# Linear attention followed by a channel mix on one core: first batch in two halves up to the channel mix, tail groups in one PSUM tile, loads in pieces

## The chip, the cores and the metric

The kernel runs on one core of a Trainium2 chip. The metric is the device time of one execution in microseconds (us). A kernel is given by the median of its runs; a ratio is the mean time of one kernel's fast runs over the mean of the other's fast runs of the same rounds on the same chip, so it is not quite the ratio of the medians that stand beside it. A run more than 1.5% above the fastest of its kernel counts as slow and is left out of ratios. Intervals are 95%.

## The reference

```python
def phi(x):                                   # q, k: [8, 8, 576, 64], w_phi: [64, 128]
    proj = x @ w_phi
    proj = proj - max(abs(proj), axis=-1)
    return concatenate([exp(proj), exp(-proj)])
kv  = phi(k).T @ v                            # per head; z = sum of phi(k) over the sequence
x   = (phi(q) @ kv) / (phi(q) @ z)            # heads side by side: [8, 576, 512]
# channel mix
x_prev = x shifted by one position
xk = mu_k * x + (1 - mu_k) * x_prev           # xr the same with mu_r
out = sigmoid(xr @ w_r) * (relu(xk @ w_k) ** 2 @ w_v)
```

There are 8 batches, and 4 pairs of heads in each, so 32 pairs; 576 positions are nine slots of 64.

## The kernel before: what the change and the argument touch

The program is a list of named steps, and one long string, ORDER, fixes their order. Each engine executes its own steps in this order. A word is `step:buffer/ENGINE+fillers`; pair numbers stand behind the name, and fillers are matmuls whose result nobody uses, placed where TensorE would stand idle. PSUM is the memory that TensorE writes its products to; a one-bank tile of this program holds 512 columns of it, a two-bank tile 1024. The granted clock is the share of TensorE's full clock that the profile shows as granted. For a pair n the chain is: `qp`, `kp` (projections on TensorE), `rq`, `rk` (maxima on VectorE), `mh` (the maxima split in two bf16 parts), `mt`, `mc` (transposed and copied), `ka`, `qt` (the maxima subtracted on TensorE), `ea`, `eb`, `qa`, `qb` (exponentials on ScalarE), `kv`, `kc`, `nd` (the two attention products), `rd` (division by the denominator, giving x_sc). From pair 8 on, x is transposed by a DMA that SyncE issues (`xz`); `xu`, `df`, `xa`, `xb` then make the shifted copy, the difference and the two mixes. `h`, `r`, `v` are the channel-mix products of a batch, `rl`, `sq`, `th`, `ob`, `so` what follows them. The ninth slots of a batch's pairs form a tail group with its own short chain: `tp`, `rt`, `mhe`, `mte`, `mce`, `kae`, `ekt`, `qte`, `eqe`.

```python
        def mhx():                                        # step mh, on GpSimd
            nc.gpsimd.tensor_copy(mhv[:, :, 0], nmv)
            nc.gpsimd.tensor_tensor(mhv[:, :, 1], nmv, mhv[:, :, 0], op=ALU.subtract)
        ...
        def eq(pn):                                       # steps qa, qb: two instructions of 512 columns each
            ...
                for h in range(2):
                    nc.scalar.activation(t[:, h, :]..., s["qT"]...[:, h], AF.Exp, scale=...)
        ...
        def xz():                                         # SyncE
            nc.sync.dma_start_transpose(out=xs[:, a, :]..., in_=s["x"]...)
        def xu(eng):                                      # GpSimd or VectorE, as ORDER says
            copy(eng, xs[:, a, 1:64], xs[:, a, 576:639])
        ...
        def mte():                                        # tail group: a one-bank tile of its own
            s["pm"] = pm = motile(("mo", "m" + tag), "ps_me")
            nc.tensor.transpose(pm[:, 0:64].bitcast(BF), mh, ident)
        def ekt():                                        # reads bank 0 of the tail group's two-bank tile
            ... nc.scalar.activation(t[:, a0:a1, :], s["ps"][:, 0, 0:n * 128]..., AF.Exp, ...)
        def qte():                                        # writes another one-bank tile
            s["pq"] = ps = motile(("mo", "q" + tag), "ps_qe")
    ...
    lparts = {b: [(0, NP)] for b in range(B)}             # whole-batch loads, from batch 2 on
```

## Time and profile before

| kernel before | value | where it is read |
|---|---|---|
| time | 305.18 us (304.40 to 307.18, 4 runs) | the runs |
| span of the profiled run | 304.2 us | page |
| TensorE idle | 25.8 us | span less busy time |
| granted clock, mean | 0.986 | trace |
| first channel-mix matmul | 51.9 us | timeline of TensorE |

Three more lines of the DMA view matter later, the last of them for pair 8's transpose alone (window 86:87 us). Its columns are output and input, queue, count, size of one, and the median time from issue to landing in us:

```profile
nat<-in_q_dram POOLq DMA_DIRECT2D x6, 576.0 KB, 8.9
xs<-x_sc SPq DMA_TRANSPOSE x24, 3.5
...
xs<-x_sc SPq DMA_TRANSPOSE x1, 2.6
```

A transpose of x takes 3.5 us in the median, and pair 8's, the first, 2.6 us: the last load issued before it had landed at 81.8 us, 4.6 us before its issue. Pair 12's took 11.0 us (issued at 120.48, landed at 131.48). The planned duration in the program text is 2.2 us (the third argument of `op("xz" + N + ".d", "DMA", 2.2, ...)`), and the order was laid out with that.

### The profile page before, as it was taken

The page shows a single profiled execution, that of the slowest core. Times are in us where ns is not written, and L with a number is a line of the kernel's source. Part 1 is how long each engine was busy: PE and PEld are TensorE (multiplying, and loading weights), DVE is VectorE, ACT ScalarE, POOL GpSimd, SP SyncE. Part 2 cuts the span into 40 slices and gives each one's busy share as a digit, 9 for nine tenths or more (in the row PEclk, how much of TensorE's full clock was granted, in tenths as well). Part 3 has the DMA queues.
Part 4 walks back from the last instruction along what each step waited for, and adds up shares of the span by engine and source line. Part 5 has one row for each costly group of instructions (what it writes and reads, how often), then busy time and mean ns, then how long its engine had stood idle before and what let it go on. Part 6 is the DMA issues. An engine that isn't in the chain of part 4 may idle for free.

```text
span 304.2 us, 9054 instructions
## 1 busy us (share of the span) xinstructions
PE 278.4 (92%) x3765; PEld 158.4 (52%) x3813; DVE 240.3 (79%) x369; ACT 223.3 (73%) x408; POOL 127.4 (42%) x261
## 2 busy tenths in 40 slices
PE   6688798999899999969999997999999999999993
PEld 2456465565456655534555654454556655554541
DVE  5776789979978999667978988799869888777331
ACT  3397899998689897855888884898797878923410
POOL 7763533696047346653443714353034403400400
PEclk9999989999999999998999999999999999999999
DMA  8999957399989957996957898913924364233125
GB/s 152 204 209 207 169 83 105 59 194 206 194 174 128 148 124 131 197 200 113 177 110 107 145 125 157 162 47 61 187 60 69 11 93 94 58 74 71 39 58 116
DMA packets 66137, 38.18 MB, mean 126 GB/s; under 512 B 47024, under 2 KB 60720, under 8 KB 66096
## 3 DMA queue, kind: packets, MB, share of 16 engines
q1 hardware_dynamic: 51280, 20.82, 39.4%
q0 software_dynamic: 14672, 16.48, 35.1%
q8 instruction: 30, 0.49, 0.7%
q10 hardware_dynamic: 144, 0.29, 0.3%
q14 instruction: 11, 0.09, 0.1%
HBM read 33.62 MB, written 9.44 MB: 142 GB/s over the span
## 4 chain that ended last, share of the span: by engine, by line
PE 61%; DVE 18%; DMA 7%; ACT 6%; issue 3%; POOL 2%; SPq 1%; DVEq 0%; POOLq 0%
PE ps_v L812 14%; PE ps_h L779 13%; PE ps_r L798 7%; PE ps_nd L656 5%; DMA xs<-x_sc 4%; PE ps_kv L635 4%; DVE nm L565 4%; DVE nm L560 3%; DVE xk L706 2%; PE ps_ve L896 2%; ACT q L620 2%; PE ps_he L866 2%; DVE xr L706 2%; PE ps_q L548 2%; PE ps_k L598 2%
## 5 line engine op out<-in xcount | busy, mean ns | idle before, releaser
L620 ACT ACTIVATE q<-ps_qT 128x512 bf16<-128x512 f32 x128 | 67.1, 622 | 3.0 <-PE ps_qT L612 2.8
L575 ACT ACTIVATE k<-ps_k 128x1024 bf16<-128x1024 f32 x64 | 62.9, 1038 | 5.6 <-PE ps_k L598 4.3
L779 PE MATMUL ps_h<-xk,wk_bf 128*128 128x512 bf16 x237 | 60.8, 379 | 1.3 <-issue 0.3
L812 PE MATMUL ps_v<-wv_bf,kk 128*128 128x512 bf16 x243 | 58.2, 379 | 1.0 <-issue 0.3
L565 DVE TENSOR_REDUCE nm<-ps_q 128x8 f32<-128x1024 f32 x32 | 38.7, 1218 | 4.3 <-PE ps_q L548 4.1
L560 DVE TENSOR_REDUCE nm<-ps_k 128x8 f32<-128x1024 f32 x32 | 38.8, 1217 | 3.8 <-PE ps_k L548 3.8
L812 PEld LDWEIGHTS <-kk 128*128 128x128 bf16 x256 | 23.9, 98 | 28.8 <-issue 1.9
L211 POOL TENSOR_TENSOR kk<-krelu 128x512 bf16<-128x512 bf16 x23 | 23.9, 1047 | 35.4 <-DVE krelu L205 21.7
L779 PEld LDWEIGHTS <-wk_bf 128*128 128x128 bf16 x256 | 22.5, 97 | 25.2 <-issue 2.3
L584 POOL CAST mhl<-nm 128x16 bf16<-128x16 f32 x32 | 8.0, 250 | 64.1 <-DVE nm L560 64.0
L798 PE MATMUL ps_r<-wr_bf,xr 128*128 128x512 bf16 x118 | 32.9, 394 | 1.2 <-issue 0.5
L804 ACT ACTIVATE rt<-ps_r 128x512 bf16<-128x512 f32 x32 | 19.5, 609 | 18.0 <-PE ps_r L798 15.7
L700 POOL TENSOR_TENSOR diff<-xs 128x576 bf16<-128x576 bf16 x21 | 28.0, 1336 | 7.6 <-DVE xs L682 2.8
L203 ACT ACTIVATE krelu<-ps_h 128x512 bf16<-128x512 f32 x39 | 23.2, 611 | 10.1 <-PE ps_h L779 8.3
L706 DVE SCALAR_TENSOR_TENSOR xk<-diff,mu_k_t,xs 128x576 bf16<-128x576 bf16 x32 | 28.5, 892 | 1.3 <-POOL diff L700 1.0
L818 DVE SCALAR_TENSOR_TENSOR ob<-rt,ps_v 128x512 f32<-128x512 bf16 x32 | 21.8, 682 | 8.7 <-PE ps_v L812 4.2
L666 DVE TENSOR_TENSOR x_sc<-ps_nd,rden 128x640 bf16<-128x640 f32 x32 | 26.4, 825 | 1.1
L706 DVE SCALAR_TENSOR_TENSOR xr<-diff,mu_r_t,xs 128x576 bf16<-128x576 bf16 x32 | 26.9, 840 | 0.0
L548 PEld LDWEIGHTS <-qkT 64*128 64x128 bf16 x512 | 17.6, 94 | 12.0 <-issue 9.7
L635 PE MATMUL ps_kv<-v,k 64*128 64x65 bf16 x1024 | 22.8, 192 | 0.6 <-ACT q L620 0.4
L635 PEld LDWEIGHTS <-k 64*128 64x128 bf16 x1024 | 19.9, 95 | 5.1 <-issue 3.8
L205 DVE TENSOR_SCALAR krelu<-ps_h 128x512 bf16<-128x512 f32 x25 | 17.1, 688 | 6.6 <-PE ps_h L779 6.0
(99 smaller groups left out, 467.5 us busy)
## 6 DMA issues: line engine op xcount, KB each, us to landing
out_dram<-ob SPq DMA_DIRECT2D x72, 128.0 KB, 2.4
nat<-in_k_dram POOLq DMA_DIRECT2D x6, 576.0 KB, 8.6
nat<-in_q_dram POOLq DMA_DIRECT2D x6, 576.0 KB, 8.9
vt<-in_v_dram POOLq DMA_DIRECT2D x6, 576.0 KB, 9.6
wk_bf<-in_moe_w_k_dram POOLq DMA_DIRECT2D x2, 512.0 KB, 10.8
wv_bf<-in_moe_w_v_dram POOLq DMA_DIRECT2D x2, 512.0 KB, 12.3
nat<-in_k_dram POOLq DMA_DIRECT2D x3, 288.0 KB, 7.4
nat<-in_q_dram POOLq DMA_DIRECT2D x3, 288.0 KB, 7.3
```

The costliest lines, as they stand in the source:

```text
L211: (nc.vector if eng == "DVE" else nc.gpsimd).tensor_tensor(out_, in_, in_, op=ALU.mult)
L560: nc.vector.tensor_reduce(s["nm"][:, 0, :], s["k"].rearrange("p a (g f) -> p (a g) f", f=128), axis=AX.X, op=ALU.max, apply_absolute_value ...
L565: nc.vector.tensor_reduce(s["nm"][:, 1, :], s["q"].rearrange("p a (g f) -> p (a g) f", f=128), axis=AX.X, op=ALU.max, apply_absolute_value ...
L575: nc.scalar.activation(s[f"k{pn}"], s["k"].rearrange("p a (g f) -> p (a g) f", f=128), AF.Exp, scale=(1.0 if pn == 0 else -1.0))
L620: nc.scalar.activation(t[:, h, :].rearrange("f (g a p) -> f g a p", g=4, a=2), s["qT"].rearrange("f a (g h p) -> f h g a p", g=4, h=2)[:, ...
L635: nc.tensor.matmul(ps[:, hh, pn * 65:(pn + 1) * 65], lhsT=s[f"k{pn}"][r, c, :], rhs=vb[r, a, 2 * g + par, :], start=(pn == 0 and c == 0), ...
L666: nc.vector.tensor_tensor(s["x"].rearrange("p (b s) d -> p b s d", b=2), ndv[:, :, :, 0:64], s["rd"].to_broadcast([128, 2, 5, 64]), op=ALU ...
L700: (nc.vector if eng == "DVE" else nc.gpsimd).tensor_tensor(s["d"], xs[:, a, 64:64 + S], xs[:, a, 0:S], op=ALU.subtract)
L706: nc.vector.scalar_tensor_tensor(out=t[:, a, (b % 2) * S:(b % 2 + 1) * S], in0=s["d"], scalar=mu[:, a:a + 1], in1=xs[:, a, 0:S], op0=ALU.m ...
L779: nc.tensor.matmul(ps, lhsT=wk_bf[:, c, fc * 128:(fc + 1) * 128], rhs=xkt[bp][:, c, m0:m0 + 512], start=(c == 0), stop=(c == NDC - 1))
L798: nc.tensor.matmul(ps, lhsT=xrt[bp][:, c, m0 + ci * 128:m0 + (ci + 1) * 128], rhs=wr_bf[:, c, :], start=(c == 0), stop=(c == NDC - 1))
L812: nc.tensor.matmul(ps, lhsT=s["kk"][:, fc, ci * 128:(ci + 1) * 128], rhs=wv_bf[:, fc, :], start=(fc == 0), stop=(fc == NFC - 1))
```

## The change

The intent was to start the channel mix earlier, by having only the first slots of the first batch done, and to free the two one-bank PSUM tiles from the tail groups. Cut to its core:

```diff
+    NHALF = NP                                  # pairs 0 to 3: qt, qa, qb, nd, rd, xt, xe, df, xa, xb twice,
+            for i, h in enumerate("yz"):        #   "y" for slots 0 to 5, "z" for slots 6 to 9
...
+        def h2(k):                              # batch 0: ps_h of 256 tokens x two blocks of features
...
-                for h in range(2):
-                    nc.scalar.activation(...)   # q exponentials: four of 512 columns in a pair
+                nc.scalar.activation(t..., s["qT"]..., AF.Exp, ...)   # two of 1024
...
         def mte():
-            s["pm"] = pm = motile(("mo", "m" + tag), "ps_me")
+            nc.tensor.transpose(s["ps"][:, 1, 0:64].bitcast(BF), mh, ident)
         def qte():
-            s["pq"] = ps = motile(("mo", "q" + tag), "ps_qe")
+            s["pq"] = ps = s["ps"][:, 1, :]     # bank 1 of the tile whose bank 0 ekt reads
...
-    lparts = {b: [(0, NP)] for b in range(B)}
+    lparts = {b: [(0, 2), (2, 4)] for b in range(B)}
...
-        op("mh" + N, "POOL", 0.5, ...)
+        op("mh" + N, "POOL", 0.5, ..., alt=("POOL", "DVE"))   # 18 of 32 pairs now name VectorE, 5 of 10 tail groups too
...
+        cols = [(0, DM)] if bp < B // 2 - 1 else [(0, DM // 2), (DM // 2, DM)]   # last ps_ve in two column halves,
+                op("soea" + nmi, "ACT", ...)                                      #   last two stores from two queues
```

The slots of "y" and "z" are numbered 1 to 9; the products have a tenth block, 0, that the halved pairs do not copy on. Some buffers grow by one to three, and the whole string ORDER is new (about 1,500 words). Counts by instruction: q exponentials 128 of 512 columns become 56 of 1024 and 16 of 512; ps_h 256 of 512 columns become 224 of 512 and 64 of 256; fillers 39 become 37; 18 more load issues on GpSimd.

## The prediction

> **What bounds the kernel now.** I read the page of the kernel before first (busy shares and the slices), then a table of busy time by stretch, then the chain of waits inside the stretches where TensorE was not full, and last the instruction timeline there.
>
> ```profile
> PE 278.4 (92%) x3765; PEld 158.4 (52%) x3813; DVE 240.3 (79%) x369; ACT 223.3 (73%) x408; POOL 127.4 (42%) x261
> PE   6688798999899999969999997999999999999993
> ...
> DMA  8999957399989957996957898913924364233125
> ```
>
> TensorE is busy for 278.4 of 304.2 us, and its row is nine tenths nearly everywhere after the seventh slice. So the time is TensorE's work plus TensorE's idle time. The next table says where that idle time lies.
>
> ```profile
> core 0: us, PE busy (x) PEld busy (x) DVE busy (x) ACT busy (x) POOL busy (x), PEclk, DMA share, GB/s
> 0.00:53.00 53.00, 41.49 (x676) 26.15 (x683) 39.96 (x77) 38.91 (x78) 28.60 (x64) 0.97 0.98 161
> ...
> 72.00:80.00 8.00, 6.96 (x94) 4.07 (x95) 7.93 (x12) 5.07 (x12) 2.79 (x4) 1.00 1.25 184
> ...
> 128.00:140.00 12.00, 9.02 (x129) 4.82 (x129) 7.57 (x11) 7.82 (x16) 6.32 (x17) 0.86 1.23 198
> ...
> 184.00:192.00 8.00, 6.40 (x73) 3.50 (x72) 7.33 (x12) 3.96 (x7) 3.45 (x6) 1.00 0.84 134
> ...
> 296.00:304.20 8.20, 3.23 (x15) 1.27 (x13) 1.38 (x2) 0.93 (x2) 0.00 (x0) 0.91 0.58 124
> ```
>
> Idle is length less PE busy: 11.5 us up to the first channel-mix matmul at 53 us, 1.0 in 72 to 80, 3.0 in 128 to 140, 1.6 in 184 to 192, 5.0 at the end; the other stretches share the rest of the 25.8. The 34 filler matmuls (12.0 us busy) lie in the head as well, so about 23 us of the first 53 do no useful TensorE work. The chain of waits names what ends the largest later gap:
>
> ```profile
> 125.10 13.39 DMA xs<-x_sc
> ```
>
> and the timeline of TensorE shows the gap itself:
>
> ```profile
> 134.53 0.23 PE L476 MATMUL ps_me<-ident,mhlt 128*128 128x128 bf16 x1 [2.44 <-POOL mhlt L471]
> ```
>
> The tail group's small maxima split on GpSimd was queued behind a copy that waited for the DMA transpose of x. In the DMA view of 110 to 140 us these transposes take this long:
>
> ```profile
> xs<-x_sc SPq DMA_TRANSPOSE x3, 11.0
> ```
>
> against a median of 3.5 us over the whole run. GpSimd had just issued five whole-batch loads of 576 KB within 10 us (117.5 to 127.7 in its timeline).
>
> **What the Trainium skill says.** "DMA: Bandwidth & Descriptors", section "Queues, rings and completion order": each DMA engine goes round robin between the queue rows it has work for, a packet at a time. The trace agrees that loads delay transposes: 11.0 us against 3.5. "TensorE: Matmul & The Clock Gate", part 1: after an idle window the array's clock falls to half and needs a busy window to return. The trace agrees: the granted clock is 0.86 in 128 to 140, after the 2.4 us gap, and 0.97 in the head although fillers were placed there. "VectorE: DVE Perf Modes", section on the TRN2 errata, gives ScalarE a fixed part per instruction, so that one wide ACTIVATE should beat two narrow ones. Here the trace says less: four 128x512 exponentials in a row took 2.06 us, two 128x1024 ones 1.94, because neighbours overlap.
>
> **The change part by part.** Counts are from the two instruction listings, durations from the rows of the page and the timeline.
>
> 1. ScalarE's q exponentials: 128 of 512 columns become 56 of 1024 and 16 of 512. 28 pairs x (2.06 - 1.94) = 3.4 us less busy. Ten more relu evictions at 0.61 and three more v copies at 0.68 go to ScalarE; two squares of krelu (0.64 each) and some small copies leave; its sum stays near 223. It was not the bound (73%).
>
> 2. VectorE: 18 of 32 maxima splits and 10 of 20 of the tail groups' move to it from GpSimd, 56 small instructions, at 0.14 each (its 8-column TENSOR_TENSOR took 0.13 to 0.15) about 8 us. Ten relu evictions (6.9) and nine squares (about 5) leave it. The halved pairs pay fixed parts twice, about 2.5 us. Net about zero, 240.
>
> 3. GpSimd: 18 more load issues at 0.74 (13 us), ten more squares at 1.05, fewer splits (about 13 less): 127 becomes about 140. Not the bound.
>
> 4. TensorE: same columns. 64 ps_h matmuls of 256 columns replace 32 of 512, fillers fall from 39 to 37. Busy stays near 278, so all gain must come from idle.
>
> 5. The head. Only the first halves of four pairs (slots up to the sixth) must be mixed before ps_h starts. I walked VectorE, ScalarE and the three two-bank tiles by hand with the trace's durations (reduction 1.22, split 0.3 to 0.5, exponential 1.0 or 0.5, copies 0.4 to 0.7) and 0.1 us per handover. Landmarks: first transposes 5.8; pair 0's split done 12.1 (11.6 before, since the tail group's split goes ahead of it); pair 0's nd 21 (25 before); all eight PE transposes copied 24 (26 before), but two reductions fewer done (2.4 us of VectorE); pair 1's first-half mix 40; pair 3's 43.6; pair 4's k reduction and split 45; pair 2's first-half mix 46.0, and ps_h at 46 to 48 against 53.0. But less is done by then. Against the order of before, one qp, one kp, one ka, one mt, two kv, two qt, one nd and one xt are still to come: 0.23+0.23+0.22+0.1+1.3+1.1+0.65+0.38 = 4.2 us of TensorE work. The fair comparison is 46 to 48 with 53.0 - 4.2 = 48.8, a gain of 0.8 to 2.8. Some is given back: from there VectorE owes two reductions, four second-half mixes, relus and a reduction more, about 11.7 us, before batch 0's second ps_h half, while TensorE has 10.4 us to do. So 1.0 us.
>
> 6. Loads in pieces. In the new order, between pair 12's transpose and batch 4's tail split, five 288 KB loads are issued (1.4 MB) in place of five of 576 KB (2.9 MB). At the 198 GB/s of that stretch this is about 7 us of traffic in place of 14.5. The margin, though, shrinks from about 14 to 10.5 us of TensorE work. The gap cost 3.0 us idle, and the clock of 0.82 in 136 to 144 another 8 x 0.18 = 1.4. I give 55% of 4.4: 2.4 us.
>
> 7. Tail groups in their own tile and more buffers: the waits at 72 to 80 and 184 to 192 were transposes behind VectorE's ob, which had to free a one-bank tile (1.55 us in one piece at 187.75). The new order no longer puts tail transposes and their q projection in these two banks. I give half of 1.0 and 1.6: 1.3 us.
>
> 8. The end: the last ps_ve in two column halves: ob 0.35 in place of 0.69, and the last two stores issued from two engines, one issue of 0.55 in place of 1.10. About 0.9 us of the 5.0.
>
> New gaps, as a wholly new order is likely to have on the chip: 1.0 us worse. Sum: -1.0 - 2.4 - 1.3 - 0.9 + 1.0 = -4.6; 305.7 - 4.6 = 301.1, said as 301.0.
>
> **The rivals.**
> First, the head is bound by VectorE and stays so: then ps_h starts near 48 but the second half starves TensorE, the head gains nothing, and the rest gives 302 to 303. For it: VectorE was busy 7.6 and 7.8 of 8 us in 40 to 56; against it: it idled about 12 us in the head, much of that behind GpSimd and ScalarE handovers that the new order takes out.
> Second, the DMA transposes come late again. The bytes are the same and DMA is at nine tenths in many slices; then the gap of 2 to 4 us is only moved, and the time is 303 to 305. For it: the margin is smaller in the new order. Against it: half the bytes in the burst.
> Third, all gaps close: TensorE dense from 47 us on, with 1 us of idle in place of about 9 after the head: 296 to 298. For it: 216 to 296 already has 79.15 of 80 busy. Against it: VectorE at 85% in 128 to 216 leaves little slack.
>
> **Range and chances.** The three rivals span 296 to 305; I take 297 to 305. Faster by over 2% means below 299.6, 1.4 us under my figure, with a spread of about 3 us either way: 0.34. Slower by over 2% means above 311.8, which needs several new gaps as large as the largest now: 0.04.
>
> **What would show it.** Right: first ps_h matmul at 46 to 48 us; TensorE busy near 278; landing time of the x transposes near pair 12 below 8 us, no gap over 2 us after the head; the last matmul to the end about 4 us. Wrong: VectorE at or over 7.8 of 8 us in 48 to 64 with TensorE below 7.4 there (first rival); a GpSimd copy again ended by a transpose of 9 us or more, with the granted clock under 0.9 (second); TensorE busy well above 280, which would mean the small pieces cost TensorE time that I counted as nothing.

## The result and the profile after

| | before | after |
|---|---|---|
| time, median (range, 4 runs each) | 305.18 us (304.40 to 307.18) | 323.69 us (318.60 to 324.54) |
| span of the profiled run | 304.2 us | 316.8 us |
| TensorE busy, idle | 278.4, 25.8 us | 284.7, 32.1 us |
| granted clock of that run | 0.986 | 0.968 |

The ratio is 1.0521 (1.040 to 1.064): slower. Two of the runs after, at 324.0 and 324.5 us, count as slow and are not in it. A later set of runs gave 321.23 us and 1.0445 (1.0355 to 1.0535); the intervals overlap. The page of the changed kernel, against the rows in the prediction:

```profile
PE 284.7 (90%) x3809; PEld 165.9 (52%) x3859; DVE 247.8 (78%) x441; ACT 226.2 (71%) x357; POOL 140.7 (44%) x239
PE   6779778999999479999899989989999989999994
...
PEclk9697979999999897999999999999999999999999
DMA  8999626099969742999989898988262423235125
```

The PE row has a hole (4) in the fourteenth slice, near 108 us. The PEclk row is below 9 in five of the first sixteen slices. The table by stretch (length, busy time of each engine, granted clock, DMA share, GB/s):

```profile
0.00:52.25 52.25, 40.76 (x544) 25.79 (x549) 41.23 (x109) 30.75 (x61) 26.05 (x52) 0.87 0.91 157
...
104.00:112.00 8.00, 3.38 (x51) 1.85 (x53) 2.83 (x8) 3.15 (x5) 4.40 (x10) 0.81 0.82 141
112.00:120.00 8.00, 6.28 (x69) 3.65 (x68) 5.38 (x8) 4.22 (x8) 0.00 (x0) 0.93 0.28 44
120.00:128.00 8.00, 7.73 (x112) 4.93 (x111) 5.82 (x10) 4.51 (x9) 4.29 (x8) 0.83 0.45 90
```

The head is as long as before (52.25 us to the first channel-mix matmul, against 51.9) at a clock of 0.87 in place of 0.97. The clock of the head differs from run to run: over the first 52 us it was 0.93 to 0.97 in the five traces with the head of before, and 0.87 to 0.97 in those with the new one. From 104 to 120 us TensorE is idle for 6.3 of 16 us. The chain of waits and TensorE's timeline name that gap:

```profile
96.94 8.40 DMA xs<-x_sc
```

```profile
108.28 0.23 PE L602 MATMUL ps_m<-ident,mhl 128*128 128x128 bf16 x1 [4.33 <-POOL mhl L598]
```

and GpSimd's timeline shows how the one makes the other:

```profile
91.57 0.76 POOL L327 DMA_DIRECT2D nat<-in_k_dram  x1
...
95.09 0.72 POOL L332 DMA_DIRECT2D vt<-in_v_dram  x1
...
105.39 0.23 POOL L210 COPY xs<-xs 128x63 bf16<-128x63 bf16 x1 [8.51 <-DMA xs<-x_sc]
...
107.72 0.21 POOL L597 CAST mhl<-nm 128x16 bf16<-128x16 f32 x1
```

Five loads of 288 KB are issued in 4.2 us. The transpose of x for pair 8, issued right behind them, lands after 8.4 us, where it took 2.6 us before. GpSimd's next step is the copy `xu8`, which needs it, so GpSimd stands for 8.51 us; pair 12's split, whose input had long been there, is the step behind, and TensorE waits 4.33 us for it. In the list of waits of TensorE a second entry is new:

```profile
PE ps_e L505 <- ACT tk L500: 6.8, 5, 1.7
PE ps_m L602 <- POOL mhl L598: 4.3, 1, 4.3
```

(total us, times, longest.) The q projection of the tail group (L505, step `qte`) waits five times for the exponential of its k part (L500, `ekt`). The two use different banks, but of one tile, and the program orders accesses by tile. Before the change `qte` had its own tile and did not wait. Pair 12's transpose, which the prediction had looked at, did land sooner than the 11.0 us of before (window 138:139 us of the change; in the second profile of the change it took 6.8 us):

```profile
xs<-x_sc SPq DMA_TRANSPOSE x1, 4.8
```

So the known kind of gap has moved from pair 12 to pair 8 and grown, and a new kind has come. The end is as foreseen: from the last matmul (312.73 us) to the end of the span 4.1 us in place of 5.0.

### The profile page after: what moved, and what is told of

Its sections match the earlier page's. A ratio compares the mean times of both kernels' runs of the same rounds, so it can differ in the third digit from the quotient of the medians.

```text
span 316.8 us, 9145 instructions
## 1 busy us (share of the span) xinstructions
PE 284.7 (90%) x3809; PEld 165.9 (52%) x3859; DVE 247.8 (78%) x441; ACT 226.2 (71%) x357; POOL 140.7 (44%) x239
## 4 chain that ended last, share of the span: by engine, by line
PE 62%; DVE 19%; ACT 7%; DMA 7%; POOL 2%; issue 2%; POOLq 0%; DVEq 0%; ACTq 0%; SPq 0%
PE ps_v L968 15%; PE ps_h L935 11%; PE ps_r L954 7%; DMA xs<-x_sc 5%; PE ps_nd L666 4%; PE ps_kv L646 3%; DVE nm L578 3%; PE ps_he L1025 2%; PE ps_ve L1061 2%; DVE nm L573 2%; PE ps_pt L344 2%; DMA nat<-in_q_dram 2%; PE ps_qT L619 2%; PE ps_k L561 2%; PE ps_q L561 2%
## 5 line engine op out<-in xcount | busy, mean ns | idle before, releaser
L632 ACT ACTIVATE q<-ps_qT 128x1024 bf16<-128x1024 f32 x56 | 55.0, 1031 | 6.4 <-PE ps_qT L625 6.2
L935 PE MATMUL ps_h<-xk,wk_bf 128*128 128x512 bf16 x207 | 52.8, 380 | 1.2 <-issue 0.5
L222 POOL TENSOR_TENSOR kk<-krelu 128x512 bf16<-128x512 bf16 x30 | 32.4, 1089 | 47.7 <-ACT krelu L214 36.6
L954 PE MATMUL ps_r<-wr_bf,xr 128*128 128x512 bf16 x116 | 32.1, 386 | 1.1 <-DVE krelu L216 0.3
L214 ACT ACTIVATE krelu<-ps_h 128x512 bf16<-128x512 f32 x45 | 27.1, 608 | 8.1 <-PE ps_h L935 6.7
L935 PEld LDWEIGHTS <-wk_bf 128*128 128x128 bf16 x224 | 19.6, 97 | 21.1 <-issue 1.1
L709 POOL TENSOR_TENSOR diff<-xs 128x576 bf16<-128x576 bf16 x20 | 25.5, 1274 | 8.7 <-DVE xs L692 4.4
L715 DVE SCALAR_TENSOR_TENSOR xk<-diff,mu_k_t,xs 128x576 bf16<-128x576 bf16 x28 | 23.1, 823 | 1.9 <-POOL diff L709 1.6
L676 DVE TENSOR_TENSOR x_sc<-ps_nd,rden 128x640 bf16<-128x640 f32 x28 | 23.1, 824 | 1.0
L210 POOL COPY xs<-xs 128x63 bf16<-128x63 bf16 x21 | 6.0, 285 | 31.2 <-DMA xs<-x_sc 31.2
L666 PE MATMUL ps_nd<-kv,q 128*128 128x65 bf16 x448 | 19.2, 195 | 0.0
```

The source lines that it names most:

```text
L222: (nc.vector if eng == "DVE" else nc.gpsimd).tensor_tensor(out_, in_, in_, op=ALU.mult)
L632: nc.scalar.activation(t.rearrange("f j (a p) -> f j a p", a=2), s["qT"].rearrange("f a (j p) -> f j a p", p=64), AF.Exp, scale=(1.0 if pn ...
L666: nc.tensor.matmul(ps[:, bk, o * 65:(o + 1) * 65], lhsT=tail if sl < 2 else s[f"q{pn}"][:, sl - 2, :], rhs=s["kv"][:, sl % 2, pn, :], star ...
L715: nc.vector.scalar_tensor_tensor(out=t[:, a, (b % 2) * S:(b % 2 + 1) * S], in0=s["d"], scalar=mu[:, a:a + 1], in1=xs[:, a, 0:S], op0=ALU.m ...
L935: nc.tensor.matmul(ps, lhsT=wk_bf[:, c, fc * 128:(fc + 1) * 128], rhs=xkt[bp][:, c, m0:m0 + 512], start=(c == 0), stop=(c == NDC - 1))
L954: nc.tensor.matmul(ps, lhsT=xrt[bp][:, c, m0 + ci * 128:m0 + (ci + 1) * 128], rhs=wr_bf[:, c, :], start=(c == 0), stop=(c == NDC - 1))
```

## The experiments

All kernels gave correct results. "Change" means the changed kernel. The diffs are of ORDER unless code is shown.

### First set: which of the two waits, and the piece size

**Pair 12's split on VectorE.**

```diff
- mh12/POOL
+ mh12/DVE
```

> The changed kernel with one word of its order altered: pair 12's maxima split runs on VectorE in place of GpSimd, where it stood behind the copy that waits for the DMA transpose of pair 8. Theory A (GpSimd's queue behind a late transpose is the largest loss): the 4.3 us wait of ps_m near 104 us goes and with it some of the half-clock time after it; 5 to 8 us less than the changed kernel, so 314 to 318 us. Rival B (the transpose is late anyhow and the next step that needs x waits as long): 0 to 2 us less.

Measured: 320.47 us, ratio 1.0404 (1.035 to 1.046). The 4.3 us wait is gone, and a wait of 5.84 us of a q projection on x_sc stands at 147 us. The interval overlaps that of the change, so this run alone shows no gain; a wait was handed on.

**Tail groups: the q projection ahead of the exponential that shares its tile.**

```diff
- kae3.0 ekt3.0 qte3.0            (the same for groups 0.2, 4.0, 5.0, 7.0)
+ kae3.0 qte3.0 ekt3.0
- eqe0.0 kae0.0                   (the same for 0.1)
+ kae0.0 eqe0.0
```

> The changed kernel with the tail groups' steps reordered so that TensorE's two writes to the shared tile come before ScalarE's two reads: no work changes. Theory C (sharing one tile makes TensorE wait for ScalarE between the two): the waits of 6.8 us (five times for tk) and 1.1 us (two times for tq) vanish and the time falls by 4 to 8 us, to about 315 to 319. If these waits only took the place of other ones: 0 to 2 us less.

Measured: 317.26 us, ratio 1.0283 (1.022 to 1.035). The entry of 6.8 us and the smaller one of 1.1 us are both gone from the list of waits. By the two ratios this is 2.4% or 7 us (1.6% by the change's later set). That it is near the sum of the waits (7.9 us) is partly chance: the first channel-mix matmul comes 3.1 us earlier (49.20), and a wait of 7.10 us of a q projection on x_sc, which the change's first profile does not have, now stands at 147.7 us.

**Both.**

> Both edits together. If A and C are separate losses, the gains add: 9 to 15 us less than the changed kernel, 308 to 314. If they overlap, not more than the larger of the two.

Measured: 312.01 us (311.23 to 314.28), ratio 1.0138 (1.008 to 1.020). So far 3.8% of the 5.2% are found. The largest wait left is again a single one, in the same manner but at pair 12's own transpose; TensorE, SyncE and GpSimd in this order:

```profile
143.40 1.04 PE L561 MATMUL ps_q<-wph,qkT 64*128 64x128 bf16 x16 [6.61 <-DVE x_sc L676]
```

```profile
115.95 11.22 SPq L359 DMA_TRANSPOSE qkT<-nat  x2
127.22 2.58 SPq L981 DMA_DIRECT2D out_dram<-ob  x4
129.91 4.34 SPq L687 DMA_TRANSPOSE xs<-x_sc  x2
```

```profile
138.39 0.23 POOL L210 COPY xs<-xs 128x63 bf16<-128x63 bf16 x1 [8.20 <-DMA xs<-x_sc]
```

SyncE needed from 115.95 to 127.17 to issue two transposes of q and k (the second took 8.3 us, where the median of the twelve in this trace is 2.8; the loads that it reads had landed by 109.2), then issued four stores, and only then pair 12's x transpose (129.91). It landed at 138.3. GpSimd waited 8.20 us for it, VectorE's mixes of pair 12 waited for GpSimd's difference, and behind them in VectorE's order stood pair 14's division, which frees the tile that the q projection needed.

**Batches 2 to 7 loaded whole, on the change itself.**

```diff
-    lparts = {b: [(0, 2), (2, 4)] for b in range(B)}
+    lparts = {b: [(0, NP)] for b in range(B)}
```

> The changed kernel with batches 2 to 7 loaded whole again (576 KB per load), each at the place of its first piece. Theory D (many small loads just ahead of the first x transposes make them late): it would be faster by 3 us or more. My prediction's view (pieces help): slower by 2 to 5 us, with transposes landing later than 9.8 us. No effect of size: within 2 us.

Measured: 323.03 us, ratio 1.0398 (1.031 to 1.049), with two of four runs slow. The interval overlaps that of the change: inconclusive. Pair 8's transpose took 7.5 us here and TensorE waited 3.45 us for pair 12's split, so large pieces do not remove the wait either.

### Second set: room for the late transpose, halves, VectorE, and parts alone

**Room at pair 12, first try.** On the kernel with both mends:

```diff
- xu12/POOL df12/POOL xa12 xb12 ... rd14 ... mhe4.0/POOL
+ xu12/POOL df12/POOL ... rd14 xa12 xb12 ... mhe4.0/DVE
```

> The kernel with the tail order and pair 12's split mended, and further: pair 12's two mixes moved on VectorE behind pair 14's rescaling (so that the x transpose of pair 12 may come late without holding the two-bank tile), and batch 4's tail split moved from GpSimd to VectorE. Theory A (in-order queues behind a late transpose are what remains): the 6.6 us wait of a q projection on x_sc near 137 us goes, with the half clock after it; 304 to 307 us, ratio 0.99 to 1.00, TensorE idle about 6 us less. Theory B (there is always a next late transpose in line, because the order has no slack anywhere): a new single wait of over 3 us shows up later, after 150 us, and the time stays at 309 to 312, ratio 1.01 to 1.02.

Measured: 313.31 us, ratio 1.0242 (1.017 to 1.032); no gain. VectorE's timeline shows that my edit had only moved the block by one instruction:

```profile
138.68 1.58 DVE L715 SCALAR_TENSOR_TENSOR xk<-diff,mu_k_t,xs 128x576 bf16<-128x576 bf16 x1 [3.27 <-POOL diff L709]
...
142.04 0.47 DVE L481 CAST mhlt<-me 128x4 bf16<-128x4 f32 x1
```

The division was now free, but the mixes stood ahead of batch 4's tail split, and TensorE waited 6.47 us for that.

**The first batch not halved**, on the same kernel.

```diff
-    NHALF = NP
+    NHALF = 0
-        halves = b == 0
+        halves = False
```

with each y/z pair of words put together at the place of the first.

> The same kernel as the one before in this list, with the first batch not halved: whole pairs of ten slots, 512-column channel-mix matmuls, the order otherwise that of the change. Theory H (the halving costs in the head: fixed parts twice on VectorE, which is near full from 40 to 56 us): 1 to 3 us faster than the halved one, first channel-mix matmul later (about 51 to 53 us) but with more useful TensorE work done by then. Theory N (the halving gives the 1 us that the prediction put on it): 0.5 to 2 us slower than the halved one.

Measured: 319.54 us, ratio 1.0428 (1.038 to 1.048), by the ratios 1.8% slower than the halved one; first channel-mix matmul at 55.35 us against 49.34. So theory H, that the halving itself costs, finds no support here. But this order was made for halves, so the difference is not what halving is worth in an order of its own.

**Six splits of the head back on GpSimd**, on the same kernel.

```diff
- mhe0.0/DVE mhe0.1/DVE mh0/DVE mh1/DVE mh3/DVE mh4/DVE
+ mhe0.0/POOL mhe0.1/POOL mh0/POOL mh1/POOL mh3/POOL mh4/POOL
```

> The first kernel of this list with the six maxima splits of the head that the change gave to VectorE (two of the tail groups, pairs 0, 1, 3 and 4) back on GpSimd. Theory V (VectorE bounds the head, so every small instruction put there costs): VectorE under 7.5 of 8 us in 40 to 48, useful TensorE work at 56 us up by 0.7 us or more, time down by 1 us or more. Rival P (the handover to GpSimd and its slower small instructions cost as much): useful work at 56 us the same or less, time the same within 1 us or longer.

Measured: 318.83 us, ratio 1.0393 (1.034 to 1.045), 1.5% slower. TensorE waits for the first tail split, which on GpSimd stands behind load issues that themselves wait:

```profile
14.38 0.29 PE L486 MATMUL ps_e<-ident,mhlt 128*128 128x128 bf16 x1 [6.51 <-POOL mhlt L482]
```

```profile
12.76 0.70 POOL L332 DMA_DIRECT2D vt<-in_v_dram  x1 [0.71 <-DMA nat<-in_k_dram]
13.45 0.20 POOL L481 CAST mhlt<-me 128x1 bf16<-128x1 f32 x1
```

The rival is right here: the early splits belong on VectorE in this order.

**Two parts of the change alone, in the order of before**: q exponentials of 1024 columns, and the end in column halves.

```diff
-                for h in range(2):
-                    nc.scalar.activation(t[:, h, :]..., ...[:, h], AF.Exp, ...)
+                nc.scalar.activation(t..., s["qT"]..., AF.Exp, ...)
- ve3:0 obe3 soe3
+ ve3.0:0 obe3.0 soe3.0 ve3.1:1 obe3.1 soeae3.1 soe3.1
```

> The kernel before, in its own order, with two parts of the change alone: each pair's q exponentials in two instructions of 1024 columns in place of four of 512, and the last output tile in two column halves with the last two stores from two queues. By the prediction: ScalarE about 3 us less busy, no gain from it as ScalarE is not the bound; 0.9 us from the end. So 304 to 305.3 where before is 305.2 to 306, ratio 0.994 to 0.998. A rival: freeing the two-bank tile sooner (the two exponentials end earlier) also closes small waits of TensorE, ratio 0.985 to 0.99.

Measured: 306.54 us (22 runs) against 306.27, ratio 0.9994 (0.997 to 1.0018). ScalarE is busy for 219.9 us in place of 223.3, as the prediction had it, and the time does not move. The expected 0.2% to 0.6% is not excluded at its small end; 1% or more is. From the last matmul to the end it is 4.6 us here, 5.0 before.

### Third set: is it the queued loads?

**Room at pair 12, second try.** On the kernel with both mends:

```diff
- xu12 df12 xa12 xb12 ... sq2.5 ... rd14 ... mhe4.0/POOL ... df13 ... mh16/POOL mc16 rd15 ... mh18/POOL
+ sq2.5 xu12 df12 ... rd14 ... mhe4.0/DVE ... mh16/DVE mc16 rd15 xa12 xb12 df13 ... mh18/DVE
```

> The change with the tail order and pair 12's split mended, and now real room for pair 12's late transpose: everything that waits for it is moved behind what TensorE needs next, on both engines (GpSimd's copy and difference behind a square; VectorE's two mixes and pair 13's difference behind pair 15's rescaling; batch 4's tail split and the splits of pairs 16 and 18 on VectorE). In the earlier attempt the two mixes had only been moved behind one instruction and still stood ahead of the tail split, whose wait became 6.5 us. Theory A (in-order queues behind a late transpose): no wait of TensorE over 2 us between 100 and 160 us, granted clock 1.0 from 136 to 152, 303 to 306 us, ratio 0.99 to 1.005. Theory B (there is always a next one): a wait of over 3 us at another instruction, 309 to 313 us.

Measured: 309.22 us, ratio 1.0099 (1.007 to 1.013). The wait is down to 2.74 us but not gone, with the clock at 0.79 from 136 to 144 us. The wait lies between the two theories, the time in the range of theory B.

**Five loads issued late**, on the kernel with both mends, where the 6.6 us wait stands:

```diff
- ... lv4.2 lq5.0 ... lk5.2 ... lv5.0 ... lq5.2 ... xu12/POOL df12/POOL
+ ... xu12/POOL df12/POOL lv4.2 lq5.0 lk5.2 lv5.0 lq5.2
```

> The change with the tail order and pair 12's split mended, in which the 6.6 us wait near 137 us stands, with one thing moved: five 288 KB loads, issued in the 10 us around pair 12's x transpose, are issued by GpSimd only after its copy that waits for this transpose. If queued loads are what makes the transpose late: it lands within 4 us of its issue (8.2 us waited before), TensorE's wait falls from 6.6 to under 2.5 us, time 305 to 309 us, ratio about 1.00. If the transpose is late for another reason (SyncE's own queue, the transposes of batch 4 ahead of it, x_sc itself): the wait stays over 5 us and the time 311 to 313 us or more, as the loads then come later too.

Measured: 307.68 us (20 runs), ratio 1.0021 (0.999 to 1.005). The 6.6 us wait is gone. SyncE issues the same transpose at 127.24, and GpSimd's copy starts at 129.87 after 1.64 us:

```profile
129.87 0.23 POOL L210 COPY xs<-xs 128x63 bf16<-128x63 bf16 x1 [1.64 <-DMA xs<-x_sc]
```

Nothing about the transpose, its engine or its reader was changed; only the loads queued near it were moved. So the queued loads make it late: issue to use is 2.6 us in place of 8.5. (Whether they delay it directly, or through the four stores issued just ahead of it on SyncE, which landed at 136.1 us with the loads there and at 127.6 without, is not separated.) The moved loads meet a later transpose, which takes 10.3 us (issued at 136.48), but no wait of TensorE over 1.8 us follows. SyncE also issues the two transposes of q and k ahead of it in 5.88 us in place of 11.22.

**The kernel before, with room at pair 12.** Nothing of the change, only this:

```diff
-                nc.gpsimd.tensor_copy(mh..., ...)
+                (nc.vector if b == 4 else nc.gpsimd).tensor_copy(mh..., ...)      # and its subtract; pair 16's split too
- xa12 sq2.5/POOL ... mh16 ... mc16/DVE xb12
+ sq2.5/POOL ... mh16 ... mc16/DVE xa12 xb12
```

> The kernel before, in its own order and with nothing of the change but this: batch 4's tail split and pair 16's split on VectorE in place of GpSimd, and pair 12's first mix moved behind pair 16's copy of the split, so that nothing that TensorE needs next stands behind the late transpose of pair 12. If the 128 to 140 us gap is that wait: its 2.4 us and the clock of 0.82 after it go, 301.5 to 303.5 us where before is 306, ratio 0.983 to 0.993. If the gap is only moved to the next instruction: ratio 0.995 to 1.005.

Measured: 305.41 us (22 runs) against 306.73, ratio 0.9935 (0.991 to 0.996): 2.0 us off the kernel before by the ratio, where 2.5 to 4.5 us were expected, and between the two stated ranges of the ratio. The trace shows the mechanism: pair 12's transpose is as late as before (10.3 us), but the tail split's transpose on TensorE (134.85 us) no longer waits for it, and the clock from 136 to 144 us is 1.00 in place of 0.82.

**The same with the two parts.**

> The previous one with the two parts of the change that cost nothing in the order of before: q exponentials of 1024 columns and the last output in two column halves. If the parts add up: 0.3 to 0.8 us under the previous one. If they were without effect: the same within 0.5 us.

Measured: 305.13 us, ratio 0.9947 (0.992 to 0.997). The two parts add nothing that these runs can see.

### Fourth set: what is left

**Late loads, and three splits on VectorE.**

```diff
- mhe4.0/POOL mh16/POOL mh18/POOL
+ mhe4.0/DVE mh16/DVE mh18/DVE
```

> The version with the five loads issued late, and besides the splits of batch 4's tail and of pairs 16 and 18 on VectorE (in its trace pair 18's split still stood on GpSimd behind a copy that waited 4.97 us for pair 15's transpose, and TensorE waited 1.75 us for it). Theory A: this wait goes, 1.5 to 2 us less than the version with the late loads alone, ratio 0.993 to 0.999. Theory B (the next late transpose takes its place): ratio 1.00 to 1.005.

Measured: 308.72 us, ratio 1.0047 (1.002 to 1.007); no gain. TensorE now waits 2.17 us at 139.2 us for batch 4's tail split: on VectorE I had left it behind a division and a reduction of a later pair.

**Seven small copies of the first batch on ScalarE, and one difference on GpSimd**, on the previous kernel.

```diff
- xfz1/DVE xez1/DVE xey1/DVE xey2/DVE mce0.2/DVE mc3/DVE mce1.0/DVE dfz1/DVE
+ xfz1/ACT xez1/ACT xey1/ACT xey2/ACT mce0.2/ACT mc3/ACT mce1.0/ACT dfz1/POOL
```

> The previous one, with seven small copies of the first batch (evictions of x for pairs 1 and 2, the split's copy of pair 3 and of two tail groups) moved from VectorE to ScalarE and one difference from VectorE to GpSimd, all between 30 and 50 us. In the mended versions VectorE runs without a gap from 27 to 58 us while ScalarE is busy 5 to 6 of 8. Theory V (VectorE bounds the head of the halved order): first channel-mix matmul about 1 us earlier (48.5 in place of 49.5), time 0.7 to 1.5 us less than the previous one. Rival W (the chain of pairs bounds it: ScalarE's copies stand behind exponentials and the mixes wait for them): the same within 0.5 us, or longer.

Measured: 310.82 us, ratio 1.0135 (1.009 to 1.018), 0.9% longer than the previous one. The first channel-mix matmul comes at 52.47 us in place of 49.88, and VectorE is busy for only 4.54 of 8 us from 32 to 40 us. TensorE has new waits for ScalarE, the longest of 1.6 us (L726, for a copy of xs).

A busy row of 7.8 of 8 had made VectorE look like the bound. This run speaks against that: with less on it the head gets longer, and the new waits are for the copies that were moved to ScalarE. It does not show that VectorE would stay harmless if the copies went elsewhere.

**Whole loads, on the version with late loads and three splits moved.**

```diff
-    lparts = {b: [(0, 2), (2, 4)] for b in range(B)}
+    lparts = {b: [(0, NP)] for b in range(B)}
```

> The one two above with batches 2 to 7 loaded whole, as before the change, in place of in two pieces of 288 KB. Theory D (small pieces keep more loads in the queues around each transpose, with 18 more issues on GpSimd): 1 to 3 us less. Rival (pieces help, as the prediction had it): 1 to 3 us more, with a GpSimd wait for a transpose of over 9 us. If piece size does nothing once the loads around pair 12 are late: the same within 1 us.

Measured: 309.82 us, ratio 1.0085 (1.0057 to 1.0113), against 1.0047 (1.0021 to 1.0073) for pieces. The intervals overlap; whether pieces help is open, and by the means it would be about 1 us.

**The kernel before with its four loads issued late.**

```diff
- lq5.0 xz12 ... lk6.0 ... lq6.0 lv6.0 ... xu12/POOL df12/POOL ... mhe4.0
+ xz12 ... xu12/POOL df12/POOL lq5.0 lk6.0 lq6.0 lv6.0 ... mhe4.0
```

> The kernel before, with nothing of the change but its four whole-batch loads around pair 12's transpose (576 KB each) issued by GpSimd only after the copy that waits for this transpose. If queued loads make the transpose late here too: pair 12's transpose lands within 6 us in place of 11, the 2.4 us wait at the tail split goes, ratio 0.988 to 0.996. If not: ratio 0.998 to 1.005.

Measured: 308.43 us, ratio 1.0033 (0.9998 to 1.0068), the profiled run slow, so its length is not compared; its order of events is. Pair 12's transpose landed 5.2 us after its issue, as expected, in place of 11.0, and the copy at 127.36 did not wait for it. But the time did not fall. TensorE's waits:

```profile
133.45 0.23 PE L476 MATMUL ps_me<-ident,mhlt 128*128 128x128 bf16 x1 [1.40 <-POOL mhlt L471]
...
149.26 3.46 PE L812 MATMUL ps_v<-wv_bf,kk 128*128 128x512 bf16 x8 [3.03 <-DVE ob L818]
```

The four issues took 3.0 us of GpSimd ahead of the split, and the loads then met the next transposes: between 143 and 147 us GpSimd waited 4.11 and 3.04 us for those of the following pairs, and a wait of 3.03 us on VectorE appeared at 149 us. Their transposes took 10.5 and 7.4 us. The cause is the same; the cure moved it.

**The change once more, for a second profile.**

> The changed kernel itself once more, for a second profile. Its first profiled run was its fastest (318.6 us; the other three 322.3 to 324.5), and showed no wait at pair 12, while all four of its mended versions did (5.8 to 7.1 us, near 140 to 150 us). If the slower runs of the change are those in which pair 12's transpose comes late as well: the profile shows, beside the waits of 4 us at pair 12's split and the 6.8 us of the tail groups, a wait of a q projection on x_sc of 5 to 7 us, in a run of 322 us or more. If the spread has another cause: no such wait, in a run of 322 us or more.

Measured: 321.23 us, ratio 1.0445; the profiled run took 320.67 us. It has the wait at pair 12's split (4.4 us), the tail groups' (6.5 us), and a third of 2.1 us for x_sc at 149 us. The third is there, but less than the 5 to 7 us of the mended versions; the spread of the change's runs is so only partly explained.

**Late loads, with the tail split directly behind its own reduction.**

```diff
- rt4.0 ... rq17 mhe4.0/POOL ... mh18/POOL
+ rt4.0 mhe4.0/DVE ... rq17 ... mh18/DVE
```

> The version with the five loads issued late, batch 4's tail split on VectorE directly behind its own reduction (in the try before it stood on VectorE behind pair 17's q reduction, for which TensorE waited 2.17 us), pair 16's split left on GpSimd and pair 18's on VectorE. If the remaining waits near 139 us are only this in-order place: no wait over 1.2 us between 100 and 160 us, 1.5 to 2.5 us less than the two tries before, ratio 0.995 to 1.000. If the order simply has the next wait in line: ratio 1.002 to 1.006 as before.

Measured: 306.28 us (22 runs) against 307.52, ratio 1.0003 (0.998 to 1.003). No wait of TensorE over 1.2 us is left between 100 and 160 us. The time lies just above the expected range, and its interval overlaps that of the late loads alone (1.0021), so the gain over that version is not shown; that the waits are gone is. So they were a matter of the in-order place and not an endless row. With these waits mended the change stands where the kernel before stands; the best version is the kernel before with room at pair 12 (0.9935), which beats both kernels.

**What the mended change still lacks.** Traces with every matmul record can be compared by the columns that TensorE has worked off (fillers left out, 64-row matmuls counted half, each matmul counted once at its start). At 96 us the three traces in the order of before have done 132,600 to 136,300 columns, three mended changes (late loads, late loads with three splits moved, and the last version) 127,900 to 129,000. At the pace of the next 8 us in the order of before, about 2,200 columns a us, the means lie 3.0 us apart; at 48 us, by the pace there (1,560), it is already 2.8. The new order's head therefore does less work in the same time. This is an estimate with a spread of 1.7 to 3.9 us, large enough for the difference between 1.0003 and 0.9935 (2.1 us). Which of its waits makes it is open: neither moving splits to GpSimd nor copies to ScalarE helped.

## Why the prediction was wrong, by its own steps

Predicted 301.0 us, range 297 to 305, with a chance of 0.04 for slower by over 2%; measured 323.7. The sum was -4.6 us; it came out at +18 us by the medians, +16 by the ratio of the fast runs. Steps 6 and 7 failed, and they explain most of it: with both mended the ratio is 1.0021.

- **Step 6, loads in pieces: the step that failed most.** It took the bytes around pair 12 as the whole matter. There it held in the change itself: pair 12's transpose landed after 4.8 and 6.8 us in the two profiles, in place of 11.0. What it left out is where the new order puts the loads. Five of them now stand right ahead of pair 8's transpose, which took 2.6 us before and takes 8.4 us now, and pair 12's split stands behind the copy that waits for it: 4.33 us of TensorE, then a clock of 0.81 to 0.93 up to 128 us. In the versions with these waits mended in part, pair 12's transpose was late too (7.8 to 9.7 us), and in three of them TensorE waited 5.8 to 7.1 us. Moving pair 12's split and the five loads takes the time from 1.0283 to 1.0021 (on two chips). The second rival named the mechanism and gave it 303 to 305 us; it priced one gap of before, moved, and not what a wait of 8 us on an in-order engine holds up behind it. (That queued loads are the cause was tested at pair 12 alone; at pair 8 it is read from the order of events.) The prediction had also read the wrong line: the transpose of 13.39 us in its chain of waits is pair 13's, which landed at 138.49, after the gap; the one behind the gap is pair 12's.
- **Step 7, tail groups in their own tile.** Counted as a gain of 1.3 us, it cost more than that. TensorE's waits for `ob`, which it meant to remove, did go (2.5 us in its list before, 0.4 after), but a wait of `qte` on `ekt` came that did not exist before (6.8 us, and 1.1 us in the opposite pair). Changing the order of the two gave about 7 us. I had looked at which bank each step used and not at which tile.
- **Step 5, the head.** The walk gave ps_h at 46 to 48 us; it came at 52.25, at 49.2 with the tail order mended, and with less work done. The point of comparison was misread as well: before, ps_h starts at 51.92 us and not at 53, so the walk's own gain was -0.3 to 1.7 us in place of 0.8 to 2.8. Two terms were too small. The 56 split instructions cost VectorE 13.3 us, not 8, as the groups below sum up with the tail groups' (2.4 and 1.6 us). And halving costs more than 2.5 us on VectorE. In the first 72 us the mixes of a halved pair take 10.2 / 4 = 2.55 us against 1.75 of a whole one, division and reciprocal 1.34 against 1.04, so 1.1 us a pair or 4.4 us in all.

```profile
L805 DVE SCALAR_TENSOR_TENSOR xk<-diff,mu_k_t,xs 128x256 bf16<-128x256 bf16 (+1 forms) x12 | 5.1, 452 | 0.0
L805 DVE SCALAR_TENSOR_TENSOR xr<-diff,mu_r_t,xs 128x256 bf16<-128x256 bf16 (+1 forms) x12 | 5.1, 448 | 0.0
```

```profile
L597 DVE CAST mhl<-nm 128x16 bf16<-128x16 f32 x18 | 6.2, 344 | 0.5
L598 DVE TENSOR_TENSOR mhl<-nm,mhl 128x16 bf16<-128x16 f32 x18 | 3.1, 175 | 0.6
```

  The test on ScalarE speaks against these two making VectorE the bound. The sign of the first rival is there for 8 us of its 16 (VectorE 7.93 and TensorE 6.74 of 8 from 48 to 56 us, 7.14 and 7.75 in the next 8). The walk's 0.1 us for a handover may be the error; that is argued, not shown, and what lengthens the head stays open.
- **Step 4, TensorE busy near 278.** It was 284.7 with about as many records missing (50 against 48). Of the 6.3 us, 3.3 are the transposes of q and k in the head, 298 ns on average in place of 222, part of them at a granted clock of 0.5 (10.0 to 16.9 us in this trace). In the second profile, with TensorE at 284.7 us too, they take 255 ns and 1.7 us more than before. The rest is not traced; it is no sign that small pieces cost TensorE time.

```profile
L344 PE MATMUL ps_pt<-ident,nat 128*128 128x128 bf16 x72 | 8.6, 298 | 1.6 <-DMA nat<-in_q_dram 0.6 <-ACT qkT L208 0.5 <-DVE nat L210 0.4
```

- **Steps 1, 3 and 8 held.** ScalarE 226 us against 223, GpSimd 140.7 against 140, 4.1 us from the last matmul to the end where about 4 was said. Step 1's claim that 3.4 us less on ScalarE buys no time was tested together with step 8: 0.9994, so step 8's shorter end bought no time that these runs can see. Step 2 was 248 against 240, by the terms named under step 5.
- **The allowance for new gaps was 1.0 us.** The two new entries in TensorE's list of waits alone are 6.8 and 4.3 us in the profiled run. A new order of 1,500 words had the whole risk of the change in it, and its allowance was one of the smallest terms of the sum.
- **The largest term looked at the right place.** The gap of before near 130 us is the late transpose, and mending it directly, with six small instructions on another engine and one mix moved, gave 0.65%. No other version tried here got more.

## What to carry to other kernels

A step that waits for a DMA holds up all steps behind it on the same engine. So ask of each such step, not only of the one that is late today, what stands behind it, how long the DMA takes while loads are queued (here 8 us and not 3), and move the needed step ahead, or the loads away, before restructuring anything. When steps are put into one tile, read the order of its readers and writers by tile, not by bank. And when an edit removes a wait without saving time, look at which instruction stands directly behind the moved one: four of the edits here had only handed the wait on.

## What the Trainium skill lacked or had wrong

- "DMA: Bandwidth & Descriptors", section "Issuing engines are not separate DMA queues", calls the time that issuing takes on a sequencer usually small relative to the DMA. Here two DMA transposes of q and k kept SyncE for 11.22 us while loads were queued and 5.88 us when five loads were moved away (issue to landing 6.7 and 10.4 us, and 4.8 and 6.3), and everything SyncE had to issue afterwards, pair 12's transpose among it, waited for that.
- The same page, section "Queues, rings and completion order", has the round robin between queues but no figure for what it does to a small transfer: 3.0 us in the median for an x transpose of the change, 8.4 us behind five loads of 288 KB.
- The same page's "Rules for kernel authors" advises to issue a DMA early and wait late. That is not free on a shared set of DMA engines: issuing five loads later took a wait of 6.6 us off TensorE, behind the readers of another transfer (ratio 1.0138 to 1.0021, on two chips), while in the order of before the same move gave nothing (1.0033).
- No page that I read says that a wait for one bank of a two-bank tile can come from the other bank's reader in a program that orders by tile: 6.8 us here, gone when the two steps changed places.
